# Splitting one weight load by partition stride, and three small edits around it, in a decode layer on one core

## The chip, the core and the metric

The kernel runs on one core of one Trainium2 chip. The metric is device time in microseconds (us) of one execution. Its engines are TensorE (PE, with its weight loads as PEld), VectorE (DVE), ScalarE (ACT), GpSimd (POOL) and SyncE (SP, which here issues nearly all DMAs). Sixteen DMA engines move the data.

## What is computed

One token goes through an attention block over a cache of 16,384 keys per head and then through a gated feed-forward block, both modulated by a condition vector. Cut to what matters:

```python
mod = silu(c) @ w_mod                       # c: 640, w_mod: 640 x 3840; six vectors sa, ca, ga, sb, cb, gb
h   = layernorm(x) * (1 + ca) + sa
q   = h @ wq                                # 32 heads x 128
p   = softmax(q . k_cache * 128**-0.5)      # per head, 16384 keys
x   = x + ga * ((p @ v_cache) @ wo)
h   = layernorm(x) * (1 + cb) + sb
out = x + gb * ((silu(h @ w_gate) * (h @ w_up)) @ w_down)    # 640 -> 1728 -> 640
```

All tensors are bf16. The two caches are 268 MB of the 290 MB that are read.

## The kernel before

**Order of the loads.** All large loads are issued by SP, in program order, as the lambda in `dma` (L90): `w_mod` (L351), `wq` (L352), the keys of pair 0 in two halves, the keys of pair 1 (after the modulation matmuls are done), then in turn the values and keys of the following pairs, then `wo` in two pieces (L640), `w_gate`, `w_up` and five pieces of `w_down` (L650 to L660). A load of keys waits for the matmuls (`o_R`) that have read the buffer two pairs earlier (`load_k`, L498); a load of values waits for `pv` of the pair before (`load_v`, L504). The 32 heads are taken as 16 pairs; one pair's keys, and its values, are 8.4 MB, 64 KB on each of 128 partitions.

**w_mod.** Its view `wm_v` lies in the second key buffer: partition p holds rows 5p to 5p+4 of `w_mod`, 38,400 contiguous bytes. One load fills all 128 partitions. All loads with the key "wm" count on one semaphore; the matmuls `f_mod` (L434) wait for its full count.

**A pair.** DVE multiplies keys by the query and folds the products (`score`, and `score_end` for the first and last pair, L567); PE adds the remaining 16 columns by matmuls with the identity (`reduce_mm` L540; `reduce_end` L580 for the first and last pair); `largest` and `weigh` make the maximum and the exponentials; `pv` (L510) multiplies by the values. The middle pairs run in a hardware loop on PE. The first pair's 256 columns of sums are made in two halves: `reduce_end(0, 0, ...)` after the first half of its keys is folded, `reduce_end(0, 1, ...)` after the second, 16 matmuls of 128 columns each.

**The end.** `project` (L680) multiplies by `wo`: for each of 32 heads one matmul of 512 columns into the tile `psb[1]` and one of 128 into `psb[6]`, on one of four column groups. ScalarE copies both row parts to SBUF (`wo_row`, L693), `f_cols` (L696) turns them into columns. A layer norm, `gate`, `up` and a chain of small DVE operations give `gu_col` (L754). `twice_gu` (L755) and `gu_half` (L757) prepare the last 64 rows of `w_down`, which only the last of the five `down` groups (L774) uses.

Of the kernel before, what the change touches and what calls it, by code (L numbers as in the profile page):

```python
# [8 lines left out]
ALU = mybir.AluOpType  # L9
ACTF = mybir.ActivationFunctionType  # L10
# [27 lines left out]
class _Plan:  # L38
# [38 lines left out]
    def op(self, eng, fn, deps=(), name="", chan=None):  # L77
        o = _Op(eng, fn, list(deps), name, len(self.ops), self.loop.get(eng), chan)
        o.sig = chan is not None
        self.ops.append(o)  # L80
        return o

    def dma(self, out_ap, in_ap, key, deps=(), name="", eng="sp", noncontig=False):
        nc = self.nc

        def fn(e, out_ap=out_ap, in_ap=in_ap, noncontig=noncontig):
            if noncontig:
                with nc.allow_non_contiguous_dma(reason="tiny vector layout change"):
                    return e.dma_start(out_ap, in_ap)
            return e.dma_start(out_ap, in_ap)  # L90

        return self.op(eng, fn, deps, name, chan=self.dma_chan(key))
# [126 lines left out]
def build(nc, A_x, A_k, A_v, A_wq, A_wo, B_wg, B_wu, B_wd, c_in, w_mod, out):  # L219
    H, S, Dh = A_k.shape[1], A_k.shape[2], A_k.shape[3]  # L220
    D = A_x.shape[2]
# [4 lines left out]
    T2 = 2 * S // 128  # L226
# [4 lines left out]
    NF = 13  # L231
# [4 lines left out]
    FCH = NF + 1  # L236
# [6 lines left out]
    with es:  # L243
        block = es.enter_context(nc.Block())
        plan = _Plan(nc, es)
        op, dma = plan.op, plan.dma
        POOL, ACT, DVE, PE = "pool", "act", "dve", "pe"

        def sb(name, shape, dtype):
            return es.enter_context(nc.sbuf_tensor(name, list(shape), dtype))  # L250

        kring = sb("kring", [128, 2, T2, 128], BF16)
# [4 lines left out]
        wm_v = kb[:, 0:KC * 6 * D].rearrange("p (k n) -> p k n", k=KC)  # L257
# [11 lines left out]
        ident = sb("ident", [128, 128], BF16)  # L269
# [43 lines left out]
        gu_col = sb("gu_col", [128, FCH], BF16)  # L313
        gu_half = sb("gu_half", [128, 2], BF16)
        even = sb("even", [128, 2], F32)
        twice = sb("twice", [128, 64, 2], BF16)
# [5 lines left out]
        wo_row = q_f[:, 0:2 * D].bitcast(F32)  # L322
# [4 lines left out]
        S_ps = psb[0]  # L327
# [6 lines left out]
        wr_ps = [psb[1], psb[6]]  # L334
        cx_ps = psb[4]
        A_ps = psb[6]
        attn_ps = psb[7]
# [8 lines left out]
        wm_src = w_mod.rearrange("(p k) n -> p k n", p=128)  # L346
# [1 line left out]
        k_src = lambda p: A_k[0, 2 * p:2 * p + 2].rearrange("h (q t) d -> (h q) t d", q=64)  # L348
        v_src = lambda p: A_v[0, 2 * p:2 * p + 2].rearrange("h (q t) d -> (h q) t d", q=64)

        d_wm = dma(wm_v, wm_src, "wm", name="dma_wmod")  # L351
        d_wq = dma(wq_v, wq_src, "wq", name="dma_wq")  # L352
        op(ACT, lambda e: e.preload_act_table_set("natural_log_exp_and_others"), name="tbl")
        d_c = dma(rows[:, 0, :], c_in, "c", name="dma_c", eng="act")
# [5 lines left out]
        o_ident = op(POOL, lambda e: e.affine_select(  # L360
            out=ident[:], in_=ones_bf[:], pattern=[[1, 128]], compare_op=ALU.is_equal,
            fill=0.0, base=0, channel_multiplier=-1), deps=[o_onesb], name="ident")
# [26 lines left out]
        def layernorm_ops(src_f32, src_dep, sum_ap, c0, tag, xc_t, free=None, between=None):  # L389
# [26 lines left out]
            out=sel[:], in_=ident[:].rearrange("p (s r) -> p r s", s=4)[:, 0:8, :], axis=AX.X, op=ALU.add), deps=[o_ident], name="sel")  # L416
        o_msk = op(DVE, lambda e: e.tensor_reduce(
            out=msk[:], in_=ident[:].rearrange("p (j k) -> p j k", k=32), axis=AX.X, op=ALU.add), deps=[o_ident], name="msk")

        def f_e32(e):  # L420
# [3 lines left out]
        o_even = op(DVE, lambda e: e.tensor_reduce(  # L424
            out=even[:], in_=ident[:].rearrange("p (j k) -> p k j", k=2), axis=AX.X, op=ALU.add), deps=[o_ident], name="even")
        o_twice = op(DVE, lambda e: e.tensor_copy(out=twice[64:128], in_=ident[64:128, 64:128].unsqueeze(2).broadcast_to([64, 64, 2])), deps=[o_ident], name="twice")
# [17 lines left out]
        def pick(half, n, o_m, free):  # L444
# [13 lines left out]
            out=tt1[:], in0=modc[:, KC:2 * KC], scalar=1.0, in1=xn[:], op0=ALU.add, op1=ALU.mult),  # L458
            deps=[o_m0, o_xn], name="t1")
# [5 lines left out]
        o_gb = op(ACT, lambda e: e.activation(out=gb_row[:], in_=mod_ps[1][:, 2 * RW:3 * RW], func=ACTF.Copy), deps=[o_mod[1], o_m1], name="gb_row")  # L465
# [5 lines left out]
        for g in range(H // 4):  # L471
            b = g % 2
# [9 lines left out]
            for half in range(2):  # L482
                ps = slice(64 * half, 64 * half + 64)
                ev.append(op(ACT, lambda e, g=g, b=b, half=half, ps=ps: e.activation(
                    out=qbc[ps, 2 * g:2 * g + 2, :],
                    in_=q_ps[b][ps, :].rearrange("p (a h d) -> p a h d", a=2, h=2)[:, :, half, :], func=ACTF.Copy),
# [80 lines left out]
        def score_end(p, c, between=None):  # L567

            kv = kring[:, p % 2, KCUT[c]:KCUT[c + 1]]
            o = op(DVE, lambda e: e.tensor_tensor(  # L570
                out=kv, in0=kv, in1=qbc[:, p, :].unsqueeze(1).broadcast_to([128, KCUT[c + 1] - KCUT[c], 128]), op=ALU.mult),
                deps=[d_k[p][min(c, len(d_k[p]) - 1)]] + o_qev[p // 2], name="mult%d_%d" % (p, c))
            for i, w in enumerate((64, 32, 16)):
                if between and i < 2:
                    between[i]()
                o = op(DVE, lambda e, w=w: e.tensor_tensor(out=kv[:, :, 0:w], in0=kv[:, :, 0:w], in1=kv[:, :, w:2 * w], op=ALU.add),  # L576
                       deps=[o], name="fold%d_%d_%d" % (p, c, w))
            return o

        def reduce_end(p, c, fold):  # L580
            def f_R(e):
                last = None
                for d in range(16):
                    last = e.matmul(S_ps[:, KCUT[c]:KCUT[c + 1]], lhsT=ident[:], rhs=kring[:, p % 2, KCUT[c]:KCUT[c + 1], d],  # L584
                                    start=(d == 0), stop=(d == 15))
                return last
            return op(PE, f_R, deps=[fold, o_ident, o_exp[p - 1] if p else o_gb], name="R%d_%d" % (p, c))

        def largest(p):
            o_pm = op(DVE, lambda e: e.tensor_reduce(  # L590
# [25 lines left out]
        load_k(0)  # L616
        load_k(1)
        load_v(0)
        reduce_end(0, 0, score_end(0, 0))
        o_R[0] = reduce_end(0, 1, score_end(0, 1))  # L620
        NLOOP = NP - 2
        for p in range(1, NP - 1):
            plan.in_loop(("pe",), "pairs", p - 1, NLOOP)
# [9 lines left out]
        PL = NP - 1  # L633
        load_v(PL)
        f0 = score_end(PL, 0, before(PL))
        reduce_end(PL, 0, f0)
        pv(PL - 1)
        wo_src = A_wo.rearrange("(p k) n -> p k n", p=128)
        WCUT = [0, 7 * H // 8, H]
        d_wo = [dma(wo_v[:, a:b, :], wo_src[:, a:b, :], ("wo", a), deps=[o_pv[PL - 1]], name="dma_wo%d" % a) for a, b in zip(WCUT, WCUT[1:])]  # L640
        diag(PL - 1)
        f1 = score_end(PL, 1)
        o_R[PL] = reduce_end(PL, 1, f1)
        largest(PL)
        weigh(PL)

# [33 lines left out]
        def project(c):  # L680

            def f_wo(e):
                last = None
                for k in range(WCUT[c], WCUT[c + 1]):
                    r = k % 4
                    for ps, a, b in ((wr_ps[0], 0, 512), (wr_ps[1], 512, D)):
                        last = e.matmul(ps[32 * r:32 * r + 32, 0:b - a], lhsT=wide(A_sb[:, k:k + 1]), rhs=wo_v[:, k, a:b],  # L687
                                        start=(k < 4), stop=(k >= H - 4), tile_position=(0, 32 * r))
                return last
            return op(PE, f_wo, deps=[o_as, d_wo[c], o_exp[NP - 2]] + o_qev[-1], name="wo%d" % c)  # L690
        for c in range(len(WCUT) - 1):
            o_p = project(c)
        o_wr = [op(ACT, lambda e, a=a, b=b, ps=ps: e.activation(out=wo_row[:, a:b], in_=ps[:, 0:b - a], func=ACTF.Copy),  # L693
                   deps=[o_p, f1], name="wo_row%d" % a) for ps, a, b in ((wr_ps[0], 0, 512), (wr_ps[1], 512, D))]

        def f_cols(e):  # L696
            last = None
# [32 lines left out]
        def gate0(o_xc1):  # L730
# [21 lines left out]
        o_sg = op(DVE, lambda e: e.tensor_tensor(out=sg[:], in0=g_sb[:], in1=rg[:], op=ALU.mult), deps=[o_rg, o_gs], name="sg")  # L752
        o_x1r = op(ACT, lambda e: e.activation(out=x1_row, in_=xr_ps[:, 0:RW], func=ACTF.Copy), deps=[o_xr], name="x1_row")
        o_gum = op(DVE, lambda e: e.tensor_tensor(out=gu_col[:], in0=u_ps[:, 0:FCH], in1=sg[:], op=ALU.mult), deps=[o_sg, o_u], name="gu")  # L754
        o_tw = op(PE, lambda e: e.matmul(attn_ps[:, 8:9], lhsT=twice[64:128].rearrange("p q h -> p (q h)"), rhs=gu_col[64:128, NF:FCH], start=True, stop=True),  # L755
                  deps=[o_gum, o_twice, o_abf], name="twice_gu")
        o_guh = op(DVE, lambda e: e.tensor_tensor(out=gu_half[:], in0=attn_ps[:, 8:9].broadcast_to([128, 2]), in1=even[:], op=ALU.mult),  # L757
                   deps=[o_tw, o_even], name="gu_half")

        for i, (b, r0, r1) in enumerate(DOWN):  # L760

            if b is None:
                work = [(gu_half[:, r // 2:r // 2 + 1], wt_v[:, RW * (r % 2):RW * (r % 2) + RW], r) for r in range(4)]
            else:
                j0 = BLOCKS[b][2]
                work = [(gu_col[:, j:j + 1], wd_v[:, j, RW * r:RW * r + RW], r) for j in range(j0 + r0, j0 + r1) for r in range(4)]

            def f_down(e, i=i, work=work):
                last = None
                for at, (col, rows, r) in enumerate(work):  # L770
                    last = e.matmul(f_ps[32 * r:32 * r + 32, 0:RW], lhsT=wide(col), rhs=rows, start=(i == 0 and at < 4),  # L771
                                    stop=(i == len(DOWN) - 1 and at >= len(work) - 4), tile_position=(0, 32 * r))
                return last
            prev = op(PE, f_down, deps=[o_gum if b is not None else o_guh, d_wd[i], o_nb[PL]], name="down%d" % i)  # L774
        o_t3 = op(DVE, lambda e: e.tensor_tensor(out=tt_row, in0=f_ps[:, 0:RW], in1=gb_row[:], op=ALU.mult), deps=[prev, o_gb], name="gb_ffn")
        o_or = op(DVE, lambda e: e.tensor_tensor(out=o_row[:], in0=tt_row, in1=x1_row, op=ALU.add), deps=[o_t3, o_x1r], name="o_row")
        o_dst = out[0, 0].rearrange("(r n) -> r n", r=4)
# [51 lines left out]
```

## Time and profile before

| | |
|---|---|
| median of 3 runs | 680.16 us (679.91 to 680.29) |
| the profiled execution | 679.98 us, of which the span is 678.2 us |
| read from HBM | 290.47 MB, 428 GB/s over the span |
| busy share of the span | PE 54%, PEld 22%, DVE 76%, ACT 7%, POOL 0% |
| granted TensorE clock, mean | 0.59 |
| queue of SP's loads (q1) | 99.2% of 16 engines' span |

The profile's page has a row of the span in 40 slices for each engine and for the DMA engines, a chain of waits that is followed back from the last instruction, groups of instructions by source line, and a list of loads with the time from issue to landing. Windows give the same busy times for any stretch; there a DMA packet is counted, with all of its time and bytes, where it starts, so that a short window can show a share over 1.

### The profile page before, as it was taken

Reading aid. Unit: us, or ns where it says so; the run is one execution under the profiler, and the core shown is the slowest. Engines: PE = TensorE matmul, PEld = TensorE weight load, DVE = VectorE, ACT = ScalarE, POOL = GpSimd, SP = SyncE. Lnnn points to the kernel's source line nnn. Section 1 sums busy time; section 2 is a strip of 40 time slices with the busy share of each in tenths; the row PEclk is TensorE's granted clock in tenths of the full one; section 3 lists DMA queues with packets and bytes.
Section 4 is the critical chain, followed back from the end, with each engine's and each line's share of the span. In section 5 each row is a group of like instructions: output and inputs, shape, how many; then the busy total and the mean of one; then the engine's idle time right before and its main releaser. Section 6 shows DMA issues by size and latency. Waiting matters only on the chain.

```text
span 678.2 us, 5410 instructions
## 1 busy us (share of the span) xinstructions
PE 366.2 (54%) x2068; PEld 146.5 (22%) x2069; DVE 513.0 (76%) x185; ACT 46.7 (7%) x147; POOL 0.7 (0%) x6
## 2 busy tenths in 40 slices
PE   2522275755728274664818375572818465471677
PEld 1111122221312122221302122121212222130236
DVE  2189997959596896959597795959699695959812
ACT  1120000100000000000000010000000000000011
POOL 0000000000000000000000000000000000000000
PEclk9675565655657565565757555575756556575765
DMA  9999999999999999999999999999999999999997
GB/s 372 442 459 433 433 433 430 433 430 433 437 430 433 433 433 433 433 437 433 433 433 433 437 433 433 433 433 433 433 433 433 433 433 433 433 437 433 434 402 305
DMA packets 6355, 290.58 MB, mean 428 GB/s; under 512 B 714, under 2 KB 972, under 8 KB 1484
## 3 DMA queue, kind: packets, MB, share of 16 engines
q1 hardware_dynamic: 6340, 290.48, 99.2%
q8 instruction: 5, 0.08, 0.0%
q10 hardware_dynamic: 8, 0.00, 0.0%
q14 instruction: 2, 0.02, 0.0%
HBM read 290.47 MB, written 0.00 MB: 428 GB/s over the span
## 4 chain that ended last, share of the span: by engine, by line
DMA 48%; DVE 28%; issue 13%; PE 11%; DVEq 0%; ACT 0%; SPq 0%
DMA kring<-in_A_k_cache_dram 45%; DVE kring L554 10%; PE psb L544 7%; DVE kring L559 6%; DVE kring L570 4%; DVE kring L576 3%; DMA vbuf<-in_A_wo_dram 3%; DVE kring L564 3%; PE psb L518 1%; PE psb L724 1%; PE psb L687 1%; PE psb L584 1%; PE psb L699 0%; PE psb L771 0%; DVE pm L590 0%
## 5 line engine op out<-in xcount | busy, mean ns | idle before, releaser
L554 DVE TENSOR_TENSOR kring<-kring,qbc 128x16384 bf16<-128x16384 bf16 x28 | 243.2, 8687 | 96.2 <-DMA kring<-in_A_k_cache_dram 96.2
L544 PE MATMUL psb<-kring,ident 128*128 x448 | 197.5, 607 | 119.3 <-DVE kring L564 119.3
L559 DVE TENSOR_TENSOR kring<-kring 128x8192 bf16<-128x8192 bf16 x28 | 123.8, 4420 | 0.5
L544 PEld LDWEIGHTS psb<-kring,ident 128*128 128x128 bf16 x448 | 53.9, 120 | 247.1 <-issue 246.0
L518 PE MATMUL psb<-vbuf,PZ 128*8 128x512 bf16 x960 | 82.6, 520 | 0.0
L594 PE MATMUL psb<-d,bd_f 128*128 128x64 f32 x32 | 11.0, 446 | 122.0 <-ACT d L592 122.0
L564 DVE TENSOR_TENSOR kring<-kring 128x4096 bf16<-128x4096 bf16 x28 | 64.0, 2286 | 0.5
L570 DVE TENSOR_TENSOR kring<-kring,qbc 128x16384 bf16<-128x16384 bf16 x4 | 34.8, 8688 | 23.4 <-DMA kring<-in_A_k_cache_dram 23.4
L518 PEld LDWEIGHTS psb<-vbuf,PZ 128*8 128x8 bf16 x960 | 27.0, 109 | 60.2 <-issue 51.5
L584 PE MATMUL psb<-kring,ident 128*128 128x128 bf16 x64 | 14.5, 392 | 40.3 <-DVE kring L576 40.3
L594 PEld LDWEIGHTS psb<-d,bd_f 128*128 128x128 f32 x32 | 8.0, 311 | 124.1 <-DVE pm L590 114.4
L576 DVE TENSOR_TENSOR kring<-kring 128x8192 bf16<-128x8192 bf16 (+2 forms) x12 | 31.7, 2645 | 0.3
L533 PEld LDWEIGHTS psb<-sel,acc_sb 128*128 128x128 f32 x128 | 28.5, 311 | 8.4 <-issue 4.3
L533 PE MATMUL psb<-sel,acc_sb 128*128 128x2 f32 x128 | 25.6, 322 | 1.4 <-ACT acc_sb L524 1.4
L524 ACT ACTIVATE acc_sb<-psb 128x512 f32<-128x512 f32 x16 | 9.6, 597 | 212.0 <-PE psb L518 212.0
L602 ACT ACTIVATE PZ<-psb,nb 64x256 bf16<-64x256 f32 x32 | 15.0, 469 | 64.8 <-DVE nb L598 64.6
L584 PEld LDWEIGHTS psb<-kring,ident 128*128 128x128 bf16 x64 | 7.4, 122 | 46.7 <-DVE kring L576 41.6
L592 ACT ACTIVATE d<-negid,pm 128x64 f32<-128x64 f32 x16 | 5.6, 348 | 153.9 <-DVE pm L590 153.9
L477 PE MATMUL psb<-vbuf,h_col 128*128 128x512 bf16 x39 | 11.2, 461 | 8.3 <-DMA vbuf<-in_A_wq_dram 8.3
L537 ACT ACTIVATE OT_sb<-psb 128x2 f32 (+1 forms) x16 | 2.8, 172 | 151.3 <-PE psb L533 151.3
L590 DVE TENSOR_REDUCE pm<-psb 128x1 f32<-128x256 f32 x16 | 6.7, 418 | 3.7 <-PE psb L584 3.7
L477 PEld LDWEIGHTS psb<-vbuf,h_col 128*128 128x128 bf16 x40 | 4.3, 116 | 15.6 <-DMA vbuf<-in_A_wq_dram 8.8
(104 smaller groups left out, 80.4 us busy)
## 6 DMA issues: line engine op xcount, KB each, us to landing
kring<-in_A_k_cache_dram SPq DMA_DIRECT2D x2, 4096.0 KB, 40.3
vbuf<-in_A_wq_dram SPq DMA_DIRECT2D x1, 5120.0 KB, 25.9
kring<-in_w_mod_dram SPq DMA_DIRECT2D x1, 4800.0 KB, 14.2
vbuf<-in_A_wo_dram SPq DMA_DIRECT2D x1, 4480.0 KB, 23.0
kring<-in_B_w_gate_dram SPq DMA_DIRECT2D x1, 2160.0 KB, 18.7
kring<-in_B_w_up_dram SPq DMA_DIRECT2D x1, 2160.0 KB, 23.5
kring<-in_B_w_down_dram SPq DMA_DIRECT2D x3, 640.0 KB, 25.7
vbuf<-in_A_wo_dram SPq DMA_DIRECT2D x1, 640.0 KB, 24.2
```

Source lines behind the costliest of these rows:

```text
L477: last = e.matmul(q_ps[b][:, 0:512], lhsT=h_col[:, k:k + 1].broadcast_to([128, 128]), rhs=wq_v[:, k, g * 512:(g + 1) * 512], start=(k == 0 ...
L518: last = e.matmul(acc_ps[32 * s:32 * s + 8, :], lhsT=PZ[:, j, :], rhs=v_at(p)[:, 4 * j:4 * j + 4, :].rearrange("p t d -> p (t d)"), start= ...
L533: last = e.matmul(OT_ps[:, 0:2], lhsT=acc_sb[:, 128 * i:128 * (i + 1)], rhs=sel[:, i:8:4], start=(i == 0), stop=(i == 3))
L544: last = e.matmul(S_ps[:, 0:T2], lhsT=ident[:], rhs=kring[:, bass.ds(plan.slot(p), 1), :, d].rearrange("p o t -> p (o t)"), start=(d == 0) ...
L554: return e.tensor_tensor(out=kv4, in0=kv4, in1=q4, op=ALU.mult)
L559: o_f = op(DVE, lambda e: e.tensor_tensor(out=kv4[:, :, 0], in0=kv4[:, :, 0], in1=kv4[:, :, 1], op=ALU.add), deps=[o_m], name="fold%d_%d" ...
L564: return op(DVE, lambda e: e.tensor_tensor(out=lo[:, :, 0:QR], in0=lo[:, :, 0:QR], in1=lo[:, :, QR:QW], op=ALU.add), deps=[o_f], name="fol ...
L570: o = op(DVE, lambda e: e.tensor_tensor(out=kv, in0=kv, in1=qbc[:, p, :].unsqueeze(1).broadcast_to([128, KCUT[c + 1] - KCUT[c], 128]), op= ...
L576: o = op(DVE, lambda e, w=w: e.tensor_tensor(out=kv[:, :, 0:w], in0=kv[:, :, 0:w], in1=kv[:, :, w:2 * w], op=ALU.add), deps=[o], name="fol ...
L584: last = e.matmul(S_ps[:, KCUT[c]:KCUT[c + 1]], lhsT=ident[:], rhs=kring[:, p % 2, KCUT[c]:KCUT[c + 1], d], start=(d == 0), stop=(d == 15))
L594: o_mx[p] = op(PE, lambda e: e.matmul(mx_ps[:, 0:64], lhsT=bd_f[:], rhs=d2[:], start=True, stop=True), deps=[o_d2, o_bd1, o_bd2, o_nb[p - ...
L602: o_exp[p] = op(ACT, lambda e, half=half, ps=ps: e.activation(out=PZ[ps, :, 4 * half:4 * half + 4], in_=S_ps[ps, 0:T2].rearrange("p (c i) ...
```

## The change

`w_mod` is loaded by four DMAs on the same semaphore key: partitions 0, 8, 16, ... (16 rows), 4, 12, ... (16), 2, 6, 10, ... (32), 1, 3, 5, ... (64). The first pair's sums are made by one group of 16 matmuls of 256 columns, after both halves are folded. `wo`'s two row parts are cut at 320 instead of 512, and the second one is copied by VectorE. `twice_gu` and `gu_half` are put behind the first `down` group.

```diff
-        d_wm = dma(wm_v, wm_src, "wm", name="dma_wmod")
+        for at, by in ((0, 8), (4, 8), (2, 4), (1, 2)):
+            d_wm = dma(wm_v[at:128:by], wm_src[at:128:by], "wm", name="dma_wmod%d" % at)
...
-        def reduce_end(p, c, fold):
+        def reduce_end(p, a, b, fold):
...
-                    last = e.matmul(S_ps[:, KCUT[c]:KCUT[c + 1]], lhsT=ident[:], rhs=kring[:, p % 2, KCUT[c]:KCUT[c + 1], d],
-                                    start=(d == 0), stop=(d == 15))
+                    last = e.matmul(S_ps[:, a:b], lhsT=ident[:], rhs=kring[:, p % 2, a:b, d], start=(d == 0), stop=(d == 15))
...
-        reduce_end(0, 0, score_end(0, 0))
-        o_R[0] = reduce_end(0, 1, score_end(0, 1))
+        score_end(0, 0)
+        o_R[0] = reduce_end(0, 0, T2, score_end(0, 1))
...
-                    for ps, a, b in ((wr_ps[0], 0, 512), (wr_ps[1], 512, D)):
+                    for ps, a, b in ((wr_ps[0], 0, D // 2), (wr_ps[1], D // 2, D)):
...
-        o_wr = [op(ACT, lambda e, a=a, b=b, ps=ps: e.activation(out=wo_row[:, a:b], in_=ps[:, 0:b - a], func=ACTF.Copy),
-                   deps=[o_p, f1], name="wo_row%d" % a) for ps, a, b in ((wr_ps[0], 0, 512), (wr_ps[1], 512, D))]
+        o_wr = [op(ACT, lambda e: e.activation(out=wo_row[:, 0:D // 2], in_=wr_ps[0][:, 0:D // 2], func=ACTF.Copy), deps=[o_p, f1], name="wo_row0"),
+                op(DVE, lambda e: e.tensor_copy(out=wo_row[:, D // 2:D], in_=wr_ps[1][:, 0:D // 2]), deps=[o_p, f1], name="wo_row1")]
...
-        o_tw = op(PE, ..., name="twice_gu")
-        o_guh = op(DVE, ..., name="gu_half")
...
             prev = op(PE, f_down, deps=[o_gum if b is not None else o_guh, d_wd[i], o_nb[PL]], name="down%d" % i)
+            if i == 0:
+                o_tw = op(PE, ..., name="twice_gu")
+                o_guh = op(DVE, ..., name="gu_half")
```

More of the change, by code (lines that the diff above doesn't have):

```diff
@@ L583, in f_R @@
                 for d in range(16):
-                    last = e.matmul(S_ps[:, KCUT[c]:KCUT[c + 1]], lhsT=ident[:], rhs=kring[:, p % 2, KCUT[c]:KCUT[c + 1], d],
-                                    start=(d == 0), stop=(d == 15))
+                    last = e.matmul(S_ps[:, a:b], lhsT=ident[:], rhs=kring[:, p % 2, a:b, d], start=(d == 0), stop=(d == 15))
                 return last
-            return op(PE, f_R, deps=[fold, o_ident, o_exp[p - 1] if p else o_gb], name="R%d_%d" % (p, c))
+            return op(PE, f_R, deps=[fold, o_ident, o_exp[p - 1] if p else o_gb], name="R%d_%d" % (p, a))
         def largest(p):
@@ L635, in build @@
         f0 = score_end(PL, 0, before(PL))
-        reduce_end(PL, 0, f0)
+        reduce_end(PL, 0, T2 // 2, f0)
         pv(PL - 1)
@@ L642, in build @@
         f1 = score_end(PL, 1)
-        o_R[PL] = reduce_end(PL, 1, f1)
+        o_R[PL] = reduce_end(PL, T2 // 2, T2, f1)
         largest(PL)
@@ L754, in build @@
         o_gum = op(DVE, lambda e: e.tensor_tensor(out=gu_col[:], in0=u_ps[:, 0:FCH], in1=sg[:], op=ALU.mult), deps=[o_sg, o_u], name="gu")
[L755 to L758, printed above, removed]
         for i, (b, r0, r1) in enumerate(DOWN):
@@ L774, in build @@
             prev = op(PE, f_down, deps=[o_gum if b is not None else o_guh, d_wd[i], o_nb[PL]], name="down%d" % i)
+            if i == 0:
+                o_tw = op(PE, lambda e: e.matmul(attn_ps[:, 8:9], lhsT=twice[64:128].rearrange("p q h -> p (q h)"), rhs=gu_col[64:128, NF:FCH], start=True, stop=True),
+                          deps=[o_gum, o_twice, o_abf], name="twice_gu")
+                o_guh = op(DVE, lambda e: e.tensor_tensor(out=gu_half[:], in0=attn_ps[:, 8:9].broadcast_to([128, 2]), in1=even[:], op=ALU.mult),
+                           deps=[o_tw, o_even], name="gu_half")
         o_t3 = op(DVE, lambda e: e.tensor_tensor(out=tt_row, in0=f_ps[:, 0:RW], in1=gb_row[:], op=ALU.mult), deps=[prev, o_gb], name="gb_ffn")
```

## The prediction

> **What bounds the kernel now.** I read the slices first, then the queues, then the chain, then single stretches. From the page:
>
> ```profile
> DMA  9999999999999999999999999999999999999997
> GB/s 372 442 459 433 433 433 430 433 430 433 437 430 433 433 433 433 433 437 433 433 433 433 437 433 433 433 433 433 433 433 433 433 433 433 433 437 433 434 402 305
> ...
> q1 hardware_dynamic: 6340, 290.48, 99.2%
> ...
> DMA 48%; DVE 28%; issue 13%; PE 11%; DVEq 0%; ACT 0%; SPq 0%
> ```
>
> The loads are the bound: 433 GB/s in every slice from the fourth to the end of the caches, the queue busy for 99.2% of the span. Engine by engine that is 433/16 = 27.0 GB/s. So whatever keeps a DMA engine busy longer before the last keys land moves the end by as much, and compute only counts after the last keys. The chain says the same: its DMA pieces are key loads.
>
> Next the start, in windows of half a microsecond (columns: length, PE, PEld, DVE, ACT, POOL busy, clock, DMA share, GB/s):
>
> ```profile
> 1.50:2.00 0.50, 0.00 (x0) 0.00 (x0) 0.43 (x3) 0.50 (x1) 0.00 (x0) 1.00 2.31 617
> 2.00:2.50 0.50, 0.00 (x0) 0.00 (x0) 0.40 (x2) 0.08 (x1) 0.00 (x0) 1.00 1.36 384
> 2.50:3.00 0.50, 0.00 (x0) 0.00 (x0) 0.13 (x1) 0.00 (x0) 0.00 (x0) 1.00 0.61 230
> 3.00:3.50 0.50, 0.00 (x0) 0.00 (x0) 0.00 (x0) 0.00 (x0) 0.00 (x0) 1.00 0.00 0
> 3.50:4.00 0.50, 0.00 (x0) 0.00 (x0) 0.00 (x0) 0.00 (x0) 0.00 (x0) 1.00 0.35 154
> 4.00:4.50 0.50, 0.00 (x0) 0.00 (x0) 0.00 (x0) 0.00 (x0) 0.00 (x0) 1.00 2.14 922
> 4.50:5.00 0.50, 0.00 (x0) 0.00 (x0) 0.00 (x0) 0.00 (x0) 0.00 (x0) 1.00 0.35 154
> ```
>
> A packet is counted where it starts. 617 GB/s x 0.5 us = 308 KB, eight rows of 38,400 B; then five (192 KB), then three (115 KB): the first row of each of the sixteen engines starts between 1.5 and 3.0. Second rows start at 3.5 to 4.0 (two), 4.0 to 4.5 (twelve), 4.5 to 5.0 (two). A later row takes 0.35 x 0.5 x 16 / 2 = 1.4 us (38,400 B at 27.0 GB/s is 1.42), a first one 2.31 x 0.5 x 16 / 8 = 2.3. Eight rows per engine make w_mod 8 x 1.42 = 11.4 us. Two things matter below: the engines move nearly in step, and the last starts about 1 us behind the first.
>
> Last the end, from the chain in order of time (start, length, what) and the list of loads:
>
> ```profile
> 658.71 4.51 PE psb L687 x64
> 663.24 0.77 ACT qbc L693 x2
> 664.02 0.04 issue
> 664.06 2.38 PE psb L699 x10
> ...
> 673.72 0.18 PE psb L755
> 673.90 2.02 PE psb L771 x30
> ```
>
> ```profile
> kring<-in_B_w_down_dram SPq DMA_DIRECT2D x1, 80.0 KB, 26.4
> ```
>
> The last w_down piece is issued at 648.9 (its row: first and last start 647.0 to 648.9) and lands 26.4 later, at 675.3; its matmuls load their weights at 675.46 on the timeline. The two ends, DMA and compute, meet within 0.1 to 0.2 us.
>
> **The change part by part**, against the profiled execution's 679.98 (the median of runs is 0.18 higher).
>
> *w_mod in four loads.* Bytes and rows stay. SP issues four instructions for one, 0.40 us each and about 0.46 apart: wq and the first keys are issued 1.4 us later. The engines have w_mod until 15 (issue 0.80 plus 14.2 to landing), so that is covered; uncovered it would cost 1.4. The gain sought can only be in the start: with one row per engine in the first load all engines may start like the first two. That is worth between 0 and the 1.0 us by which the last lags; I take 0.4, what separates the middle twelve from the first two.
>
> The cost is what the trace doesn't show. Every large load there fills all 128 partitions; none fills every eighth. If the 27 GB/s are the engine's own, a load of 16 rows costs nothing. If they belong to a sixteenth of the partitions written, two engines that write into one group at once get half each: 1.42 us more per row, for two 16-row loads 2.84, for all eight rows of an engine 11.4. So the bounds are 0 and +11.4. I take the upper end. The nearest rows are the keys' and w_mod's: the rate is the same 433 for rows of 38,400 and 65,536 B and for different sources, which looks like a limit on the side that all of them share, and what they share is that they fill all partitions. In the old load an engine's eight rows could be any partitions that have one path to themselves. In the new loads rows are dealt out anew, one, one, two and four per engine, and a stride only suits a group of eight consecutive partitions; for groups made of shorter runs it puts two engines on one group, and since engines move in step they stay there for row after row. [...] Sum: +11.4 - 0.6 - 0.4 = +10.4.
>
> [...]
>
> That w_mod lands later (about 25) delays the modulation and the issue of the second pair's keys from 19 to about 30; wq and the first keys keep the engines until then and beyond (second half of the first keys: landing at about 47 before). No further cost.
>
> *First pair's sums in one go.* Takes out 32 matmuls of 128 columns (two groups of 3.63 us, L584) and puts in 16 of 256, 7.07 us by the same form of L544. The sums end at 70.3 + 7.1 = 77.4 instead of 73.96. DVE reads them at 78.79: 1.4 us of cover. SP issues the third pair's keys at 77.4 instead of 73.99; the first values, issued at 38.87, take 47.5 and land at 86.4, so the engines have work for 9 us. Nothing is queued on SP behind it that could go sooner. Cost 0; without that cover 3.4.
>
> *wo's rows.* The 64 matmuls have the same 640 columns per head: 0. The copies: now 0.77 (0.60 for 512 columns, 0.27 for 128, overlapping). New: ScalarE with 320 columns between its rows 0.30 (160) and 0.60 (512), about 0.43; VectorE with 320 between 0.32 (160) and 0.66 (480), its row of 320 is 0.48, beside it and with VectorE idle. So 0.3 earlier for f_cols. What is late next: the last w_down piece, which leaves 0.1 to 0.2. Net -0.1 (0 to -0.3).
>
> *twice_gu.* The matmul (0.18, about 0.1 of which delays the next) is behind 16 matmuls instead of ahead of them, and the same PE work lies between gu_col and the end: 0, at most 0.1 either way. gu_half is ready 1 us before its use still.
>
> Sum: 679.98 + 10.4 - 0.1 = 690.3; with the 0.18 to the median, **690.4 us**. Its own range is 688.5 to 691.3 (relief 0 to 1.2, start 0 to 1.0).
>
> **Rivals.** *The rate is the engine's own* (or stride and groups suit each other): no sharing. For it: every packet in the trace goes at one rate, which an engine's own limit explains as well. Then -0.4 - 0.1: 679.5, with the median's offset 679.7, not slower. It decides if the two 16-row loads take no longer than two rows, 2.8 us.
> *Only the two 16-row loads share*, the other two spread over all groups: +2.84 - 0.4 - 0.1: 682.3, 682.5 to the median. [...]
> *More is won than 0.2%* (1.36 us): the whole 1.0 of the start and 0.3 at the end give 678.9; it needs something on top. Between 42 and 44 us a single packet of the instruction queue (q8) runs on one of the engines, which is out for that time; 32 fewer PE instructions may shift such fetches, by up to about 1 us: 678.
>
> **How the numbers follow.** Sharing throughout 0.45; sharing in the first two loads, or in part, 0.13; no sharing 0.33; more won 0.09. No sharing against sharing is nearly even, because no row decides it. The range leaves out the last case and 0.04 above: 679.0 to 691.3. About 0.2% is what a measurement of this kernel can tell from no change; faster by more 0.09, within 0.33, slower by more 0.58.
>
> **What would show it.** w_mod's landing: 15 to 25 us if shared, 17.5 to 18 if in two loads, 14.5 to 15 if not. The rate in the first two slices, 372 and 442 GB/s before, would fall towards 230 and 330 and the rest stay at 433. f_cols should start 0.3 earlier after the last wo matmul; the last down matmuls should wait for a DMA. The prediction is wrong if w_mod lands by 15, or if it lands late and the end does not follow by the same amount.

## The result and the profile after

The changed kernel takes 683.08 us (682.89 to 683.16, six runs) against 680.24 before: ratio 1.0042, 95% interval 1.0032 to 1.0053, slower by 2.84 us. The profiled execution took 682.89 with a span of 681.2. The time lies inside the stated range, but not near the forecast of 690.4. It lies 0.6 above the second rival's 682.5: the whole price of that rival, 2.84, without the gain of 0.5 that it also counted.

The page's rows of DMA share and rate and the lines of queue and chain that answer to those of before:

```profile
DMA  9999999999999999999999999999999999999997
GB/s 318 427 453 435 431 435 428 431 435 427 431 435 431 431 431 431 435 435 431 431 431 431 431 439 439 443 435 435 435 431 435 431 435 435 431 431 435 431 404 304
...
q1 hardware_dynamic: 6388, 290.48, 99.1%
...
DMA 45%; DVE 30%; issue 13%; PE 11%; SPq 0%; ACT 0%; DVEq 0%
```

The first slice falls from 372 to 318 GB/s and the second from 442 to 427; after that the rate is what it was. So the loss is made once, at the start: a slice is 17.03 us, and 54 GB/s x 17.03 us = 0.92 MB, 15 GB/s x 17.03 us another 0.26 MB, together 1.18 MB, which at 433 GB/s is about 2.7 us.

The same windows at the start (columns as in the prediction; the last two are DMA share and GB/s):

```profile
2.00:2.50 0.50, 0.00 (x0) 0.00 (x0) 0.39 (x2) 0.08 (x1) 0.00 (x0) 1.00 3.03 691
2.50:3.00 0.50, 0.00 (x0) 0.00 (x0) 0.13 (x1) 0.00 (x0) 0.00 (x0) 1.00 1.85 461
3.00:3.50 0.50, 0.00 (x0) 0.00 (x0) 0.00 (x0) 0.00 (x0) 0.00 (x0) 1.00 0.32 77
...
4.50:5.00 0.50, 0.00 (x0) 0.00 (x0) 0.00 (x0) 0.00 (x0) 0.00 (x0) 1.00 2.12 463
5.00:5.50 0.50, 0.00 (x0) 0.00 (x0) 0.00 (x0) 0.00 (x0) 0.00 (x0) 1.00 2.81 614
...
7.50:8.00 0.50, 0.50 (x2) 0.41 (x2) 0.30 (x2) 0.00 (x0) 0.00 (x0) 1.00 2.49 768
```

As in the prediction, share x 0.5 us x 16 engines over the number of packets is the time of one. Second rows, those of the second load, start from 4.5 on: six in one window, eight in the next, at 2.12 x 8 / 6 = 2.8 us and 2.81 x 8 / 8 = 2.8 us each. That is twice 1.42, to within 0.03. Third rows, the first of the 32-row load, start while late engines are still in the second load: 2.49 x 8 / 10 = 2.0 us. Then it is over. A window further on, in the same view:

```profile
9.50:10.00 0.50, 0.00 (x0) 0.00 (x0) 0.35 (x2) 0.11 (x1) 0.00 (x0) 1.00 2.31 998
```

998 x 0.5 / 38.4 is thirteen packets, 2.31 x 8 / 13 = 1.42 us each: the second row of the 32-row load, at full rate. Added up per engine: first packets start 0.4 later (from 2.0 on instead of 1.5), first rows take about 0.5 more, second rows 1.4, third rows 0.5: 2.8. So 2.4 of the 2.8 are slower rows, and 0.4 is the later start.

The loss goes to the end unchanged. The matmuls of w_mod wait until 18.1 instead of 15.1, and in the chain of waits the multiplication of the last keys starts later. Before, then after:

```profile
608.87 8.69 DVE kring L570
```

```profile
573.01 38.73 DMA kring<-in_A_k_cache_dram
611.73 0.02 issue
611.76 8.69 DVE kring L572
```

That is 2.89 later, and the store of the output is 2.90 later:

```profile
676.57 0.33 SPq L90 DMA_DIRECT2D out_dram<-o_row  x1
```

```profile
679.47 0.33 SPq L90 DMA_DIRECT2D out_dram<-o_row  x1
```

Nothing after the last keys gained or lost in the sum.

### The profile page after: what moved, and what is told of

Read it like the earlier page. It is cut to its first block, busy times and chain, and to the rows that moved or that the text cites. A ratio compares the mean times of both kernels' runs of the same rounds, so it can differ in the third digit from the quotient of the medians.

```text
span 681.2 us, 5383 instructions
## 1 busy us (share of the span) xinstructions
PE 362.5 (53%) x2052; PEld 143.7 (21%) x2053; DVE 513.5 (75%) x186; ACT 46.4 (7%) x146; POOL 0.7 (0%) x6
## 4 chain that ended last, share of the span: by engine, by line
DMA 45%; DVE 30%; issue 13%; PE 11%; SPq 0%; ACT 0%; DVEq 0%
DMA kring<-in_A_k_cache_dram 45%; DVE kring L556 10%; PE psb L546 7%; DVE kring L561 6%; DVE kring L572 5%; DVE kring L578 5%; DVE kring L566 3%; PE psb L520 1%; PE psb L725 1%; PE psb L688 1%; PE psb L586 1%; SPq L90 0%; PE psb L767 0%; PE psb L700 0%; DVE pm L591 0%
## 5 line engine op out<-in xcount | busy, mean ns | idle before, releaser
L546 PEld LDWEIGHTS psb<-kring,ident 128*128 128x128 bf16 x448 | 53.9, 120 | 248.5 <-issue 247.7
L520 PE MATMUL psb<-vbuf,PZ 128*8 128x512 bf16 x960 | 80.1, 507 | 0.0
L586 PE MATMUL psb<-kring,ident 128*128 128x128 bf16 (+1 forms) x48 | 14.3, 464 | 46.2 <-DVE kring L578 46.2
L586 PEld LDWEIGHTS psb<-kring,ident 128*128 128x128 bf16 x48 | 5.6, 122 | 53.8 <-DVE kring L578 46.9
L440 PE MATMUL psb<-kring,silu_c 128*32 128x480 bf16 x40 | 4.2, 604 | 8.9 <-DMA kring<-in_w_mod_dram 8.9
```

Source lines behind the costliest of these rows:

```text
L520: last = e.matmul(acc_ps[32 * s:32 * s + 8, :], lhsT=PZ[:, j, :], rhs=v_at(p)[:, 4 * j:4 * j + 4, :].rearrange("p t d -> p (t d)"), start= ...
L546: last = e.matmul(S_ps[:, 0:T2], lhsT=ident[:], rhs=kring[:, bass.ds(plan.slot(p), 1), :, d].rearrange("p o t -> p (o t)"), start=(d == 0) ...
L586: last = e.matmul(S_ps[:, a:b], lhsT=ident[:], rhs=kring[:, p % 2, a:b, d], start=(d == 0), stop=(d == 15))
```

## The experiments

Each is compared with the kernel before, on the same chip. Three theories of the start were tried against each other: G, that the partitions fall into groups of which each is written at 27 GB/s (433/16) at most, so that a load which reaches half of them makes two engines share (which partitions make a group, and so how many groups a load reaches, was assumed and is not shown); L, that each further load costs the engines something; S, that a row is slow where an engine has few rows in a load.

**The four loads alone**, the other edits undone.

```diff
+        for at, by in ((0, 8), (4, 8), (2, 4), (1, 2)):
+            d_wm = dma(wm_v[at:128:by], wm_src[at:128:by], "wm", name="dma_wmod%d" % at)
```

> The kernel before with the four loads of w_mod alone; the sums, the copies of wo's rows and twice_gu stay as before. Theory G (two engines at one group of partitions while a 16-row load runs): +2.8 to +3.2, the whole of the change's +2.84 or a little more, w_mod landing at 18.0 to 18.2 as in the changed kernel, second rows taking 2.8 us. Rival O (the other three edits bring a part of the loss, through the later sums or the wait for w_down): less than +2.

Measured: 682.99 against 680.20, +2.79, ratio 1.0041 (1.0025 to 1.0056). The loads account for the loss. Their last one is issued at 2.7 and lands 15.0 later, at 17.7, a little before the 18.0 to 18.2 that were expected.

**The other three edits alone**, w_mod in one load.

```diff
-        for at, by in ((0, 8), (4, 8), (2, 4), (1, 2)):
-            d_wm = dma(wm_v[at:128:by], wm_src[at:128:by], "wm", name="dma_wmod%d" % at)
+        d_wm = dma(wm_v, wm_src, "wm", name="dma_wmod")
```

> The changed kernel with w_mod in one load again: the other three edits alone. Theory G: -0.1 (-0.3 to +0.1), because 0.3 is won at the copies of wo's rows and most of it is waited for at the last piece of w_down. Rival O: +0.5 to +2.8.

Measured: 680.03 against 680.20, ratio 0.9997 (0.9988 to 1.0006): not to be told from no change. Its chain ends like this:

```profile
648.77 26.01 DMA kring<-in_B_w_down_dram
674.78 0.04 issue
674.82 1.06 PE psb L766 x22
675.88 0.03 issue
675.91 0.34 DVE qbc L775
676.25 0.02 issue
676.27 0.24 DVE o_row L776
```

The end hangs on the third of the five pieces of w_down, issued at 648.77; the down matmuls wait 0.45 for it. The third pair's keys are issued at 77.19 instead of 73.99, and nothing follows from it.

**Every fourth partition, fewer loads.**

```diff
+        for at, to, by in ((0, 128, 4), (2, 128, 4), (1, 128, 2)):
+            d_wm = dma(wm_v[at:to:by], wm_src[at:to:by], "wm", name="dma_wmod%d" % at)
```

> The kernel before with w_mod in three loads of every fourth, fourth and second partition (32, 32 and 64 rows), so that no load reaches only half of the groups. Theory G: no row at 2.8 us, w_mod landing at 15.0 to 15.5, time 0 to +0.4 (issue of the loads). Rival L (each further load costs the engines about 0.95 us, a third of 2.84, whatever its rows): +1.9, w_mod landing at 17. Rival S (a row is slow where an engine has few rows in a load): between, about +1.

Measured: 680.40 against 680.20, ratio 1.0004 (0.9995 to 1.0013). L's +1.9 is out, and S has no room for its +1. The second rows, windows as above:

```profile
4.00:4.50 0.50, 0.00 (x0) 0.00 (x0) 0.00 (x0) 0.00 (x0) 0.00 (x0) 1.00 2.18 922
4.50:5.00 0.50, 0.00 (x0) 0.00 (x0) 0.00 (x0) 0.00 (x0) 0.00 (x0) 1.00 0.72 307
```

Twelve and four packets, 2.18 x 8 / 12 = 1.45 and 0.72 x 8 / 4 = 1.44 us: no sharing.

**The same sizes, contiguous.**

```diff
+        for at, to, by in ((0, 16, 1), (16, 32, 1), (32, 64, 1), (64, 128, 1)):
+            d_wm = dma(wm_v[at:to:by], wm_src[at:to:by], "wm", name="dma_wmod%d" % at)
```

> The kernel before with w_mod in four loads of contiguous partitions: 0 to 15, 16 to 31, 32 to 63, 64 to 127; as many rows in each load and as many loads as in the change. Rivals L and S (number of loads, or rows of an engine in a load): +2.8 to +3 as in the change. Theory G with groups that are 8 consecutive partitions: 2, 2, 4 and 8 groups reached, rows of 11 us in the first two loads, more than +20. Theory G with groups made of shorter runs: 4, 4, 8 and 8 groups, rows of 5.7, 5.7, 2.8 and 2.8 us, so 8.5 + 2.8 + 5.7 = +17, w_mod landing at about 32. [...]

Measured: 696.71 against 680.20, +16.5, ratio 1.0241 (1.0226 to 1.0257); w_mod's last load, of 2400 KB, took 29.1 us to land (the list of loads), at about 31. The second load's rows start in these windows:

```profile
6.00:6.50 0.50, 0.00 (x0) 0.00 (x0) 0.00 (x0) 0.00 (x0) 0.00 (x0) 1.00 4.66 538
6.50:7.00 0.50, 0.00 (x0) 0.00 (x0) 0.00 (x0) 0.00 (x0) 0.00 (x0) 1.00 3.36 387
```

Seven and five packets, 4.66 x 8 / 7 = 5.3 and 3.36 x 8 / 5 = 5.4 us, 3.8 times 1.42: on theory G, about four engines at one group. As many loads with as many rows as in the change cost nearly six times as much, so it is which partitions a load fills, and not how many. Groups of eight consecutive partitions are out as well: they would put eight engines at each of two groups, rows of 8 x 1.42 = 11 us. The counts of 4, 4, 8 and 8 groups in the expectation were assumed; no run shows a group by itself. The times agree with them: 5.3 us a row in the second load, taken to reach four, and 207 GB/s from 13 to 31 us, half of 433, in the two loads taken to reach eight. One thing the runs leave open: partition p always gets rows 5p to 5p+4 of w_mod, so a load that fills other partitions also reads other places in HBM. No kernel here moved the one without the other, so that the limit lies on the side of the partitions is not shown.

**Twice the cost.**

```diff
+        for at, to, by in ((0, 128, 8), (4, 128, 8), (2, 128, 8), (6, 128, 8), (1, 128, 2)):
+            d_wm = dma(wm_v[at:to:by], wm_src[at:to:by], "wm", name="dma_wmod%d" % at)
```

> The kernel before with w_mod in five loads: partitions 0, 8, ..., then 4, 12, ..., then 2, 10, ..., then 6, 14, ... (16 rows each) and every second one from 1. Twice the suspected cost: four loads that reach half of the groups instead of two. Theory G: four rows per engine at 2.8 instead of 1.42 us, +5.5 to +5.9. Rival (a cost of the first two loads alone, as a start that small loads do not fill): +2.8 to +3.2 as in the change.

Measured: 685.86 against 680.12, +5.74, ratio 1.0082 (1.0067 to 1.0098). So it is not a matter of the start: the third and fourth loads are as slow as the second one of the change. Rows of the third load start from 7.0 on, those of the fourth from 10.0 on, and two windows among them show

```profile
7.50:8.00 0.50, 0.40 (x2) 0.31 (x2) 0.27 (x3) 0.00 (x0) 0.00 (x0) 1.00 2.46 538
10.50:11.00 0.50, 0.00 (x0) 0.00 (x0) 0.47 (x3) 0.00 (x0) 0.00 (x0) 1.00 2.48 538
```

Seven packets each, 2.46 x 8 / 7 = 2.8 and 2.48 x 8 / 7 = 2.8 us.

**Every second partition of one half, in the sizes that cost nothing.**

```diff
+        for at, to, by in ((0, 64, 2), (64, 128, 2), (1, 128, 2)):
+            d_wm = dma(wm_v[at:to:by], wm_src[at:to:by], "wm", name="dma_wmod%d" % at)
```

> The kernel before with w_mod in three loads: even partitions below 64, even partitions from 64 on (32 rows each), odd partitions (64 rows). The same number of loads, of the same sizes, as the three loads of every fourth, fourth and second partition, which cost +0.2; only which partitions they fill differs. Theory G (contiguous loads showed that partitions 64 to 127 are served at half the rate): two loads of two rows per engine at 2.8 instead of 1.42, +5.5 to +5.9. Rival (rows per engine or loads decide): +0.2.

Measured: 686.06 against 680.12, +5.94, ratio 1.0087 (1.0072 to 1.0103). Beside the every-fourth kernel this is the cleanest pair: 32, 32 and 64 rows in both, +0.2 against +5.9. The rate over the two 32-row loads (last column; the every-fourth kernel has 410 in both windows):

```profile
2.00:8.00 6.00, 0.00 (x0) 0.00 (x0) 0.52 (x2) 0.08 (x1) 0.00 (x0) 1.00 1.08 230
8.00:14.00 6.00, 1.70 (x14) 1.47 (x14) 1.90 (x11) 1.21 (x8) 0.00 (x0) 1.00 1.07 243
```

**The end without its cover.** Two kernels leave out a fifth of w_gate's load, 1.0 us, so that the pieces of w_down are early against compute. The second also has the three other edits.

```diff
-        d_wg = dma(wg_v, B_wg.rearrange("(p k) n -> p k n", p=128), "wg", deps=wdeps, name="dma_wg")
+        d_wg = dma(wg_v[:, 0:4, :], B_wg.rearrange("(p k) n -> p k n", p=128)[:, 0:4, :], "wg", deps=wdeps, name="dma_wg")
```

> The kernel before, with the last fifth of w_gate not loaded (442 KB, 1.0 us of all engines, left out; gate then uses what lies in the buffer). It makes the last w_down piece land 1.0 us earlier against compute. Both theories of the end: -0.1 to 0, because compute sets the end of the kernel before.

> The same with the three other edits (sums in one go, wo's rows on two engines, twice_gu later) and w_mod in one load; the last fifth of w_gate is not loaded here either. If the 0.3 us of wo's rows are hidden by the last w_down piece: now they show, -0.3 to -0.4 against the kernel before, 0.3 less than the other short-gate kernel, and no wait for w_down in the down matmuls. Rival (the copies win nothing, or are lost in another wait): as the other short-gate kernel.

Measured: 679.15 and 679.73 against 680.12, ratios 0.9991 (0.9982 to 1.0000) and 0.9994 (0.9985 to 1.0003). The first kernel was to win at most 0.1; its median is 0.97 lower, about the DMA time that was left out, though its interval still touches no change. Its eleven runs spread from 678.78 to 680.44, the 21 of the kernel before from 679.75 to 680.48: the shortest became 1.0 shorter, the longest did not. The second kernel was to be 0.3 to 0.4 faster than the kernel before; it reads 0.39, which its interval does not tell from no change. It was also to be 0.3 faster than the first one, and reads 0.58 slower, with intervals that overlap.

The profiles tell why a difference of 0.3 can't be seen here: compute after the last keys is not the same length in each execution. In the profile of the first short-gate kernel `gu_col` starts at 671.83, in that of the kernel before at 673.49, with the same code. The down matmuls of the first one wait 0.21 for a piece of w_down even so, and those of the kernel before do not wait at all. So either may end last: a load where compute is short, compute where it is long. That this holds for the runs without a profile is inferred from their spread and not shown. The 64 matmuls with wo, on the timelines of before, after and the three edits alone:

```profile
658.71 4.47 PE L687 MATMUL psb<-vbuf,A_sb 128*32 128x512 bf16 x64 [0.29 <-ACT A_sb L675]
```

```profile
662.22 3.79 PE L688 MATMUL psb<-vbuf,A_sb 128*32 128x320 bf16 x64 [0.29 <-ACT A_sb L676]
```

```profile
658.38 2.37 PE L687 MATMUL psb<-vbuf,A_sb 128*32 128x320 bf16 x64 [0.29 <-ACT A_sb L675]
```

The granted clock over these stretches was 0.50, 0.62 and 1.00. The time at which the clock is high differs between the profiles (from 655 to 660 us it was 0.76 before and 1.00 with the three edits alone, from 660 to 665 it was 0.50 and 0.88), and the 64 matmuls take 4.47 us in the one and 2.37 in the other. It is not the new cut of their columns: with the old one they took 3.38 us at a clock of 0.68 in the first short-gate kernel. Where they are as short as 2.37, a w_down piece decides. What the copies of wo's rows are worth with nothing behind them stays open.

**A small first load that fills all partitions.**

```diff
+        for at, to in ((0, 1), (1, 5)):
+            d_wm = dma(wm_v[:, at:to, :], wm_src[:, at:to, :], "wm", name="dma_wmod%d" % at)
```

> The kernel before with w_mod in two loads that both fill all 128 partitions: the first fifth of each partition's 38,400 B, then the rest. It has what the change was after, a small first load, without a load that reaches only a part of the partitions. If a small first load lets the engines start sooner: -0.4 (to -1.0), first packets all within 0.3 us. If the start is set by the issue and by what the first packets wait for, whatever their size: 0 (-0.2 to +0.2).

Measured: 679.93 against 680.10, ratio 0.9998 (0.9989 to 1.0007). In the window from 1.5 to 2.0 eight packets of 7,680 B start (125 x 0.5 / 7.68), as eight of 38,400 B did before, and the others follow later. A small first load wins nothing that can be measured. No way of loading w_mod that was tried is faster than one load beyond its interval.

## Why the prediction was wrong, point by point

*What bounds the kernel.* Right. 2.8 us more for the engines in the first 20 us are 2.84 at the end, and so for the other kernels: by the issue and landing of its last load, w_mod lands 2.7, 5.7, 5.8 and 16.3 later with the four loads alone, five loads, every second partition of one half and contiguous partitions, and the time is 2.79, 5.74, 5.94 and 16.5 longer.

*That loads of some partitions make engines share.* Right, as far as the runs go: rows take 2.8 us in loads of every eighth partition and 5.3 in one of sixteen consecutive partitions, where those of all partitions or of every fourth take 1.42 to 1.45. That engines share a group there is the reading of theory G. Whether the groups are of partitions or of places in HBM the runs do not separate.

*The size: this step failed.* "it puts two engines on one group, and since engines move in step they stay there for row after row" charged all eight rows of an engine, 11.4. Only the 16-row loads are slow, 2.8 us a row in the second one. The loads of 32 and 64 rows have rows of 1.42 us once the 16-row loads are through. By the count, two rows at 2.8 in place of eight cost 2.76; in the trace the rows lost 2.4 and the start 0.4, and the term of +10.4 measured +2.8. That this comes so near to the rival's 2.84 is in part luck, since the count has no later start in it. The first two slices say the same: 318 and 427 GB/s, where 230 and 330 were expected of sharing throughout. The prediction took the upper of two bounds on an argument about how engines walk through the rows that no row of the trace carried; the simple count, how many groups a load is taken to reach, gives the time of every way of loading w_mod tried here within 0.5 us, and it was the second rival's. How the rows of a load are dealt to the engines stays open: the runs show only that no row is slow (1.44 and 1.45 us) where a load fills every fourth partition. The range of its own that the prediction gave this sum is also off: 690.4 less 0.6 of relief and 0.6 of the start is 689.2, not 688.5. No run shows the 0.6 of relief itself: the second rows took 2.8 us each, within 0.03 of twice 1.42.

*The gain at the start, -0.4.* Wrong in sign. SP took about 0.59 us to issue each load and not 0.40, first packets came 0.4 later, and wq was issued at 3.35 and not at 2.7, which was covered as expected. The kernel with a small first load of all partitions shows no gain either.

*Sums in one go.* Right: the load after them is 3.2 later in the kernel with the three edits alone, and the time is the same.

*wo's rows.* The copies are as costed: 0.44 and 0.49 us side by side instead of 0.77. But the matmuls behind them start 0.71 after the last wo matmul instead of 0.89, so 0.18 and not 0.3 is won there. Before, then after:

```profile
664.06 2.37 PE L699 MATMUL psb<-ind,qbc 128*128 128x1 f32 x10 [0.89 <-ACT qbc L693]
```

```profile
666.73 2.33 PE L700 MATMUL psb<-ind,qbc 128*128 128x1 f32 x10 [0.71 <-DVE psb L707]
```

The time did not show it. With the three edits alone a piece of w_down comes later; that a load would take most of the gain was foreseen, but as the last piece and with compute always ending last in the kernel before. The short-gate kernels suggest that in some executions of the kernel before the load ends last already.

*twice_gu.* Not tried alone; with the other two it is within 0.12%.

## What to carry to other kernels

Where the DMA engines are the bound, ask of each load which partitions it fills, not how many bytes or rows it has: here loads of every eighth partition, or of every second partition of one half, ran at about half rate (246 GB/s in the four loads alone and 230 to 243 in the kernel with halves, where loads of every fourth had 410), and the next load's rows started later (in the kernel with five loads the third one's from 7.0 on, the fourth one's from 10.0). Splitting into loads that fill all 128 partitions (-0.17 us), or every fourth and every second one (+0.20), cost nothing that could be measured; a stride of eight, or every second partition of one half, cost about 1.4 us for each row of an engine (+2.79 for two rows, +5.74 and +5.94 for four). And a chain from one profile can name compute as last where a load lands 0.1 to 0.2 us ahead, as in the kernel before: make the load shorter and look at the spread of the runs, since both may end last in turn.

## What was not expected of the hardware

A load of every eighth, fourth or second partition took SP 0.54 to 0.60 us to issue, the single load of all 128 in order 0.40, and the four loads of contiguous partitions 0.40 to 0.53. Where the first load was a strided one, its first packet started 0.3 to 0.4 later (from 2.0 on in the windows); where it was 16 contiguous rows, it started from 1.5 on, as before. So it is not the number of rows in the first load that costs this; the stride, in the partitions and in the rows of w_mod alike, is what differs.

The view of the w_mod loads in the changed kernel:

```profile
L90 SPq DMA_DIRECT2D kring<-in_w_mod_dram x4: 569/588/602, 0.8 to 2.7; - x4
```
